# Attention with a gate behind it: the gate's transposes of xs and of its logits issued after the scores, its product one step sooner

## The chip, the cores and the metric

One NeuronCore of a Trainium2 chip runs the whole program. The metric is device time in microseconds (us), lower is better; a kernel's time is the median over its runs.

## The reference, cut to what matters

The program is a windowed attention with 32 global tokens per batch, followed by a mixture of experts. Only the attention and the gate's logits touch the change.

```python
s_g  = scale * q_g @ concat(k_g, k_l).T        # global queries see all keys
out_g = softmax(s_g) @ concat(v_g, v_l)
s_ll = where(|i - j| <= 32, scale * q_l @ k_l.T, -1e9)
s_l  = concat(scale * q_l @ k_g.T, s_ll)       # local queries: window + global keys
out_l = softmax(s_l) @ concat(v_g, v_l)
x = concat(out_g, out_l) as (4608, 512)        # 8 batches, 8 heads, 512 + 32 rows, head size 64
logits = x @ w_gate                            # (4608, 8)
# tokens are assigned to 8 experts greedily by logit, 576 each; out = relu(x @ w1[e]) @ w2[e]
```

## The kernel before

**Attention in steps.** The list `steps` has 40 entries of two units each (the two heads of a pair). A batch b has four local steps 5b to 5b+3 and one global step 5b+4; in the last batch, b = 7, the global step stands second (step 36). The loop of line 468 issues, for each step i, what STEADY (line 415) lists: S, the scores of step i+2 (line 215, or 286 for a global step); T0 and T1, the transposes ("turns") of the probabilities p of step i on TensorE (line 182), each with its copy from PSUM to SBUF on ScalarE (`take`, evac class "p"); M0 and M1, mask and row minimum on VectorE and the exp on ScalarE for step i+2; O0 and O1, the products with v of step i-1 (line 191) and their normalisation on VectorE into `xs[b]`; and G, whatever `extra` holds for the step. Each engine runs its own instructions in this order.

**The gate.** For each batch, `xs[b]` (128 x 4 x 512) is transposed in four groups of four 128x128 turns (`gate_x`, line 318), each group into one PSUM tile and from there copied to `xt` on VectorE (evac class "x"). `gate_m` (line 325) multiplies `xt` by the gate's weights (TensorE, eight instructions), and ScalarE copies the product to `ltc` (class "l"). `gate_l` (line 334) turns `ltc` back (four turns), and VectorE sums four partial results into the logits `L`. All these stand in G, behind O1: with s0 = 5(b+1), the groups of xs in steps s0 to s0+3, the product in s0+4, the turns of the logits in s0+5. Batch 6 (`fast`) has its groups in pairs in steps 35 and 36, its product in step 37 and its logits in 38. Batch 7 has an order of its own. `turn_xg` does the same for the global rows, in G of step s0+1.

**PSUM.** Eight banks: three tiles named S (scores), three named T and two named O. T serves the turns of p (one per unit in a local step, two per unit in a global one), the gate's groups, its product and the turns of the logits, `turn_xg`, and, when the scores of a global step are made, also the small score block `sb` of its second unit (line 290: one S and one T). This `sb` is read by M1's reduction and exp of that step. A T tile goes to a bank whose former tile has had its last reader issued, and the first write then waits for that reader.

**Loads and stores.** They are issued by `piece` (line 437) from the SyncE queue, at a pace set by the estimated work of TensorE (`tick`) and by `now_`, the position within the step; each waits for the last TensorE instruction issued before it. After attention the routing and the expert matmuls follow, which need all logits.

Of the kernel before, what the change touches and what calls it, by code (L numbers as in the profile page):

```python
# [13 lines left out]
ALU = mybir.AluOpType  # L14
AX = mybir.AxisListType
# [4 lines left out]
S = SL + SG  # L20
# [25 lines left out]
@with_exitstack  # L46
def block(ctx, tc, A, out, nbatch=B, dump=None):
    nc = tc.nc
    ctx.enter_context(tc.manual_schedule())
    consts = ctx.enter_context(tc.tile_pool(name="consts", bufs=1))  # L50
    dram = ctx.enter_context(tc.tile_pool(name="dram", bufs=1, space=DRAM))
    xd = dram.tile([N, DM], F32, name="xd")

    ident = consts.tile([128, 128], F32, name="ident")
    L = consts.tile([128, 34, E], F32, name="L")
    if dump is not None:
        nc.vector.memset(L, 0.0)
    rt = Routing(tc, A, consts, L, ident) if out is not None else None
    if rt:
        rt.begin(ctx)  # L60
    attention(tc, A, consts, xd, ident, L, nbatch, rt)
    if dump is not None:
        nc.sync.dma_start(dump["L"], L.rearrange("p a b -> p (a b)"))
        nc.sync.dma_start(dump["x"][:nbatch * S], xd[:nbatch * S])
    if out is not None:
        rt.begin_ps(ctx)
        experts(tc, A, xd, ident, rt, out)
# [3 lines left out]
def attention(ctx, tc, A, consts, xd, ident, L, nbatch, rt=None):  # L71
    nc = tc.nc
# [238 lines left out]
    def evac(dst, src, k):  # L311
        nev[k] += 1
        if who[k][nev[k] % len(who[k])] == "A" and not (k == "p" and nev[k] <= 2):
            nc.scalar.activation(dst, src, AF.Copy)
        else:
            nc.vector.tensor_copy(dst, src)

    def gate_x(src, xt, c, spare):
        t = ps.tile([128, NB, 128], F32, name="S" if spare else "T", bufs=3 if spare else 3)
        n = src.shape[1]  # L320
        for k in range(n):
            pe.transpose(t[:, k, :], src[:, k, c * 128:(c + 1) * 128], ident)
        evac(xt[:, c, :n * 128], t[:, :n].rearrange("p a b -> p (a b)"), "l" if late[0] else "x")

    def gate_m(xt, n):
        lt = ps.tile([128, 512], F32, name="T", bufs=3)
        for c in range(4):
            pe.matmul(lt[32 * c:32 * c + 32, :n * 128], wg[:, c, :], xt[:, c, :n * 128],
                             start=True, stop=True)
        ltc = wk.tile([128, 512], F32, name="ltc", bufs=2)  # L330
        evac(ltc[:, :n * 128], lt[:, :n * 128], "l")
        return ltc

    def gate_l(ltc, J, n):
        t = ps.tile([128, NB, 4, 32], F32, name="T", bufs=3)
        for k in range(n):
            pe.transpose(t[:, k].rearrange("p a b -> p (a b)"), ltc[:, k * 128:(k + 1) * 128], ident)
        nc.vector.tensor_reduce(L[:, J:J + n, :], t[:, :n, :, 0:8].rearrange("p k c e -> p k e c"),
                                axis=AX.X, op=ALU.add)

    def gate_d(xt, c):
        if c == 0:
            lt.append(ps.tile([128, NB, E], F32, name="T", bufs=3))
        for k in range(NB):
            pe.matmul(lt[0][:, k], xt[:, c, 128 * k:128 * k + 128], wg[:, c, 0:E], start=(c + k == 0), stop=(c + k == 6))
        if c == 3:
            nc.scalar.activation(L[:, 4 * nbatch - 4:4 * nbatch], lt[0], AF.Copy)
# [3 lines left out]
    def gate_units(b, src, J, n):  # L351
        xt = []

        def go(c):
            if c == 0:
                xt.append(wk.tile([128, 4, 128 * n], F32, name=f"xt{n}", bufs=1))
            if c < 4:
                gate_x(src(), xt[0], c, b == nbatch - 1)
            elif b == nbatch - 1:
                gate_d(xt[0], c - 4)  # L360
            elif c == 4:
                xt.append(gate_m(xt[0], n))
            else:
                gate_l(xt[1], J, n)
        return [lambda c=c: go(c) for c in range(8 if b == nbatch - 1 else 6)]

    late = [False]
    gxt = {}

    def turn_xg(b):  # L370
        if b % 4 == 0:
            gxt[b // 4] = wk.tile([128, 4, 128], F32, name="xt1", bufs=1)
        t = ps.tile([128, NB, 128], F32, name="S" if b == nbatch - 1 else "T", bufs=3)
        pe.transpose(t[:, 0, :], xg[b].rearrange("p a b -> p (a b)"), ident)
        q = 32 * (b % 4)
        evac(gxt[b // 4][:, :, q:q + 32], t[:, 0].rearrange("p (a b) -> p a b", a=4), "l" if late[0] else "x")

    def gate_g(i):
        gxt[i] = gate_m(gxt[i], 1)
# [8 lines left out]
    extra = {}  # L388

    def put(i, slot, f):  # L390
        extra.setdefault((i, slot), []).append(f)
    for b in range(nbatch):
        last = b == nbatch - 1
        s0 = 5 * (b + 1)
        put(s0 - 2 if last else s0 + 1, 0, lambda b=b: turn_xg(b))
        if b % 4 == 3:
            put(s0 - 1 if last else s0 + 3, 0, lambda b=b: gate_g(b // 4))
            put(s0 if last else s0 + 4, 0, lambda b=b: gate_l(gxt[b // 4], 32 + b // 4, 1))
        lo = gate_units(b, lambda b=b: xs[b], 4 * b, NB)
        if last:  # L400
            put(s0 - 3, 0, lo[0])
            put(s0 - 1, 0, lo[1])
            put(s0, 0, lo[2])
            for f in [lo[4], lo[3]] + lo[5:]:
                put(s0, 2, f)
        else:
            fast = b == nbatch - 2
            for k in range(4):
                put(s0 + (k // 2 if fast else k), 0, lo[k])
            put(s0 + (2 if fast else 4), 0, lo[4])  # L410
            put(s0 + (3 if fast else 5), 0, lo[5])

    LA = 2
    RAMP = 2
    START, STEADY = "T0 T1 O0 O1 S M0 M1 G", "S T0 T1 M0 M1 O0 O1 G"

    need, left = {}, {}
    for i, u in enumerate(steps):
        for q in [u[0].q] if isinstance(u[0], Local) else range(NP):
            for f, t in ((load_qk, i - LA), (load_v, i + 1)):  # L420
                k = f, u[0].b, q
# [8 lines left out]
    def used(f, u):  # L430
        for q in [u[0].q] if isinstance(u[0], Local) else range(NP):
            left[f, u[0].b, q] -= 1
            live[f] -= left[f, u[0].b, q] == 0

    now_ = [-LA]
# [32 lines left out]
    for i in range(-LA, ns + 1):  # L468
        if rt and i == 4:
            rt.load()  # L470
        if rt and i == 9:
            rt.prepare()
        nx = steps[i + LA] if i + LA < ns else []
        cur = steps[i] if 0 <= i < ns else []
        old = steps[i - 1] if i > 0 else []
        if i < RAMP:
            order = START
        else:
            order = STEADY
        late[0] = i >= ns - 1  # L480
        for n, what in enumerate(order.split()):
            now_[0] = i + n / 8
            if what == "S" and nx:
                (local_scores if isinstance(nx[0], Local) else glob_scores)(nx)
                used(load_qk, nx)
            if what[0] == "T" and cur:
                cur[int(what[1])].turn()
                cur[int(what[1])].take()
            if what[0] == "M" and nx:
                nx[int(what[1])].mask()  # L490
                nx[int(what[1])].exp()
            if what[0] == "O" and old:
                old[int(what[1])].out()
                if what[1] == "1":
                    used(load_v, old)
                old[int(what[1])].norm()
            if what == "G":
                if rt and i == ns:
                    for _ in first:
                        pass  # L500
                    rt.digits(slice(0, 28))
                for slot in range(3):
                    for f in extra.get((i, slot), []):
                        f()


WARM = 10
# [789 lines left out]
```

## Time and profile before

| | us |
|---|---|
| median of 3 runs | 689.69 (685.83 to 692.7) |
| profiled execution, its own time | 693.05 |
| its span, first to last instruction | 691.3 |
| PE (TensorE) busy | 644.5 (93%) |
| DVE (VectorE) busy | 460.0 (67%) |
| ACT (ScalarE) busy | 307.4 (44%) |
| POOL (GpSimd) busy | 247.7 (36%) |

Attention takes the span's first 200 us or so; the rest is routing and experts. In the profile, PE is TensorE's matmuls and PEld its weight loads; a transpose is a matmul with `ident`. "T<-ident,p" are the turns of p, "T<-ident,xs" those of xs, "T<-xt,wg" the gate's product, "T<-ident,ltc" the turns of the logits. "[0.47 <-ACT pgt]" behind an instruction is idle time of its engine just before it and what ended it; "issue" is idle time in which the engine waited for nothing that the profile shows. "x8" is a run of eight merged instructions. In such a run the duration is from the first start to the last end, and matmuls overlap, so the distance between two starts says how long a group holds TensorE.

### The profile page before, as it was taken

What the parts mean: (1) busy time and instruction counts of PE and PEld (TensorE: products, weight loads), DVE (VectorE), ACT (ScalarE), POOL (GpSimd) and SP (SyncE); (2) the same over time, 40 slices, a digit from 0 to 9 for tenths busy, and PEclk for the clock granted to TensorE, in tenths of its full rate; (3) what the DMA queues carried; (4) which work ended last, traced back from release to release, by engine and by line L of the source; (5) the groups of instructions that cost most, each with busy time, mean ns of one, the idle gap of its engine ahead of it and who ended that gap; (6) DMA issues with size and microseconds to landing.
All of it is one profiled execution on the core that took longest, in us unless ns stands there. A gap on an engine that the chain in (4) does not pass through costs nothing.

```text
span 691.3 us, 24695 instructions
## 1 busy us (share of the span) xinstructions
PE 644.5 (93%) x10358; PEld 539.5 (78%) x10358; DVE 460.0 (67%) x1765; ACT 307.4 (44%) x828; POOL 247.7 (36%) x313
## 2 busy tenths in 40 slices
PE   7898999999973799999999999999999999999996
PEld 6576777776762698779879879878978978988985
DVE  4688888788776699778758758767767772640410
ACT  5777867876720252443433324334333342542410
POOL 4687767786500311511421331141151133412011
PEclk9999999999985799999999999999999999999999
DMA  8677778876210531713240450361343146431001
GB/s 252 192 241 221 228 227 249 256 212 185 90 68 2 186 124 42 287 47 109 84 168 18 153 190 33 126 197 53 122 125 129 45 142 214 163 127 49 14 15 51
DMA packets 41119, 93.91 MB, mean 136 GB/s; under 512 B 5424, under 2 KB 28208, under 8 KB 36912
## 3 DMA queue, kind: packets, MB, share of 16 engines
q0 software_dynamic: 10240, 51.39, 21.5%
q1 hardware_dynamic: 30768, 40.95, 19.5%
q8 instruction: 81, 1.33, 0.8%
q14 instruction: 30, 0.25, 0.1%
HBM read 74.49 MB, written 17.83 MB: 134 GB/s over the span
## 4 chain that ended last, share of the span: by engine, by line
PE 89%; DVE 4%; issue 3%; DMA 2%; ACT 1%; SPq 0%; POOL 0%; POOLq 0%; ACTq 0%
PE H L1127 28%; PE Y L1086 27%; PE T L90 11%; PE S L90 7%; PE O L90 7%; PE R L630 4%; PE H L965 2%; PE Y L1094 2%; DMA qk<-in_qk_dram 1%; DVE r_pm L552 1%; DMA mask<-in_mask_dram 1%; DMA xg<-xd,idx 0%; DVE r_G L552 0%; DVE r_ce L552 0%; DMA out_dram<-y,idx 0%
## 5 line engine op out<-in xcount | busy, mean ns | idle before, releaser
L1127 PE MATMUL H<-xh,w1h 128*128 128x272 f32 (+2 forms) x512 | 151.1, 295 | 2.4 <-ACT xh L970 2.0
L1127 PE MATMUL H<-xh,w1l 128*128 128x272 f32 (+2 forms) x512 | 150.4, 294 | 0.0
L1127 PE MATMUL H<-xl,w1h 128*128 128x272 f32 (+2 forms) x512 | 149.7, 292 | 0.1
L975 POOL DMA_INDIRECT out_dram<-y,idx x40 | 41.4, 1036 | 183.3 <-ACT y L1074 102.8
L1086 PE MATMUL Y<-w2l,hh 128*128 128x512 f32 x256 | 103.3, 403 | 0.8 <-issue 0.8
L1129 ACT ACTIVATE hh<-H 128x272 fp32r<-128x272 f32 (+2 forms) x128 | 50.8, 398 | 119.7 <-PE H L1127 117.0
L1086 PE MATMUL Y<-w2h,hh 128*128 128x512 f32 x256 | 104.0, 406 | 0.0
L1086 PE MATMUL Y<-w2h,hl 128*128 128x512 f32 x256 | 103.4, 404 | 0.0
L1127 PEld LDWEIGHTS H<-xh,w1h 128*128 128x128 f32 x512 | 97.0, 189 | 3.9 <-ACT xh L970 2.1
L1127 PEld LDWEIGHTS H<-xl,w1h 128*128 128x128 f32 x512 | 97.0, 189 | 1.0 <-DVE xl L552 0.4
L1127 PEld LDWEIGHTS H<-xh,w1l 128*128 128x128 f32 x512 | 97.0, 189 | 0.4
L126 POOL COPY vw<-vw 32x650 f32<-32x650 f32 x96 | 69.4, 723 | 51.6 <-DMA vw<-in_vw_dram 36.1
L180 ACT ACTIVATE p<-p,nm 128x128 f32<-128x128 f32 x256 | 78.0, 397 | 8.1 <-DVE nm L175 8.1
L1074 ACT ACTIVATE y<-Y 128x512 f32<-128x512 f32 (+1 forms) x40 | 21.3, 534 | 123.7 <-PE Y L1086 80.3
L552 DVE SCALAR_TENSOR_TENSOR hl<-H,hh 128x272 fp32r<-128x272 f32 (+2 forms) x128 | 55.1, 434 | 30.3 <-ACT h L1131 18.5
L175 DVE CUSTOM_DVE_ANT_0 p<-S,mask 128x128 f32<-128x128 f32 x256 | 56.5, 286 | 23.3 <-PE S L90 21.8
L90 PE MATMUL S<-qk 64*32 64x128 f32 (+2 forms) x2240 | 52.6, 293 | 9.5 <-issue 5.1
L552 DVE TENSOR_TENSOR w2l<-w2r,w2h 128x512 fp32r<-128x512 f32 x64 | 42.8, 682 | 25.3 <-ACT w2h L931 25.3
L918 POOL DMA_INDIRECT xg<-xd,idx x40 | 43.3, 1082 | 38.1 <-DVE idx L552 23.8
L1086 PEld LDWEIGHTS Y<-w2h,hh 128*128 128x128 f32 x256 | 48.2, 188 | 10.4 <-issue 1.4
L1086 PEld LDWEIGHTS Y<-w2h,hl 128*128 128x128 f32 x256 | 48.2, 188 | 9.8 <-issue 0.5
L1086 PEld LDWEIGHTS Y<-w2l,hh 128*128 128x128 f32 x256 | 48.2, 188 | 9.5 <-issue 0.4
(179 smaller groups left out, 1116.9 us busy)
## 6 DMA issues: line engine op xcount, KB each, us to landing
qk<-in_qk_dram SPq DMA_DIRECT2D x64, 204.0 KB, 2.9
vw<-in_vw_dram SPq DMA_DIRECT2D x64, 162.5 KB, 3.4
xd<-xs SPq DMA_DIRECT2D x28, 256.0 KB, 3.5
qk<-in_qk_dram SPq DMA_DIRECT2D x32, 200.0 KB, 3.0
xd<-xs SPq DMA_DIRECT2D x1, 1024.0 KB
xg<-xd,idx POOLq DMA_INDIRECT x40
out_dram<-y,idx POOLq DMA_INDIRECT x40
vw<-in_ve_dram SPq DMA_DIRECT2D x32, 16.2 KB, 3.0
```

Source lines behind the costliest of these rows:

```text
L90: s.last = op(o, w, x, **kw)
L126: copy(bv[32 * g:32 * g + 32], av[32 * g + 32:32 * g + 64])
L175: nc.vector.tensor_tensor_reduce(s.p[:, c, :], s.st[:, c, :], mask[:, c, :], -SCALE, BIG, ALU.add, ALU.min, s.nm[:, c:c + 1])
L180: nc.scalar.activation(s.p[:, c, :], s.p[:, c, :], AF.Exp, bias=s.nm[:, c:c + 1], scale=-1.0)
L552: return op(*args, **kw)
L630: s.nc.tensor.matmul(out, *args, **kw)
L918: nc.gpsimd.indirect_dma_start(out=dst, out_offset=None, in_=src, element_offset=off, in_offset=bass.IndirectOffsetOnAxis(ap=idx, axis=0))
L975: nc.gpsimd.indirect_dma_start(out=out4 if t == 4 else out, out_offset=bass.IndirectOffsetOnAxis(ap=rt.idx[ph][:, k:k + 1], axis=0), in_=y ...
L1074: nc.scalar.activation(y, p[:, :w], AF.Copy)
L1086: nc.tensor.matmul(p, h[:, f, q], w[f], start=(f + k == 0), stop=(f + k == 9))
L1127: nc.tensor.matmul(p, w[d][:, fs], x[:, d, q], start=(d + k == 0), stop=(d + k == 5))
L1129: nc.scalar.activation(hh[:, f, q], p, AF.Relu)
```

## The change

The order of a step becomes S X T0 T1 M0 Y M1 O0 O1 G. At X the turns of a group of xs, or of the logits, are issued on TensorE; their copy (or sum) on VectorE is returned as a function and called at Y, between the masks of the two units. The product of a batch moves from G of step s0+4 to G of s0+3, and the turns of the logits from G of s0+5 to X of s0+4. In batch 6 the first group of each pair goes to X and the second stays in G; its logits are turned at X of step 38. The position `now_` is counted in tenths of a step instead of eighths.

```diff
--- before.py
+++ after.py
@@ -320,7 +320,8 @@
         n = src.shape[1]
         for k in range(n):
             pe.transpose(t[:, k, :], src[:, k, c * 128:(c + 1) * 128], ident)
-        evac(xt[:, c, :n * 128], t[:, :n].rearrange("p a b -> p (a b)"), "l" if late[0] else "x")
+        k = "l" if late[0] else "x"
+        return lambda: evac(xt[:, c, :n * 128], t[:, :n].rearrange("p a b -> p (a b)"), k)
 
     def gate_m(xt, n):
         lt = ps.tile([128, 512], F32, name="T", bufs=3)
@@ -335,8 +336,8 @@
         t = ps.tile([128, NB, 4, 32], F32, name="T", bufs=3)
         for k in range(n):
             pe.transpose(t[:, k].rearrange("p a b -> p (a b)"), ltc[:, k * 128:(k + 1) * 128], ident)
-        nc.vector.tensor_reduce(L[:, J:J + n, :], t[:, :n, :, 0:8].rearrange("p k c e -> p k e c"),
-                                axis=AX.X, op=ALU.add)
+        return lambda: nc.vector.tensor_reduce(L[:, J:J + n, :], t[:, :n, :, 0:8].rearrange("p k c e -> p k e c"),
+                                               axis=AX.X, op=ALU.add)
 
     def gate_d(xt, c):
         if c == 0:
@@ -355,13 +356,13 @@
             if c == 0:
                 xt.append(wk.tile([128, 4, 128 * n], F32, name=f"xt{n}", bufs=1))
             if c < 4:
-                gate_x(src(), xt[0], c, b == nbatch - 1)
+                return gate_x(src(), xt[0], c, b == nbatch - 1)
             elif b == nbatch - 1:
                 gate_d(xt[0], c - 4)
             elif c == 4:
                 xt.append(gate_m(xt[0], n))
             else:
-                gate_l(xt[1], J, n)
+                return gate_l(xt[1], J, n)
         return [lambda c=c: go(c) for c in range(8 if b == nbatch - 1 else 6)]
 
     late = [False]
@@ -406,13 +407,13 @@
         else:
             fast = b == nbatch - 2
             for k in range(4):
-                put(s0 + (k // 2 if fast else k), 0, lo[k])
-            put(s0 + (2 if fast else 4), 0, lo[4])
-            put(s0 + (3 if fast else 5), 0, lo[5])
+                put(s0 + (k // 2 if fast else k), 0 if fast and k % 2 else "X", lo[k])
+            put(s0 + (2 if fast else 3), 0, lo[4])
+            put(s0 + (3 if fast else 4), "X", lo[5])
 
     LA = 2
     RAMP = 2
-    START, STEADY = "T0 T1 O0 O1 S M0 M1 G", "S T0 T1 M0 M1 O0 O1 G"
+    START, STEADY = "T0 T1 O0 O1 S M0 M1 G", "S X T0 T1 M0 Y M1 O0 O1 G"
 
     need, left = {}, {}
     for i, u in enumerate(steps):
@@ -479,7 +480,12 @@
             order = STEADY
         late[0] = i >= ns - 1
         for n, what in enumerate(order.split()):
-            now_[0] = i + n / 8
+            now_[0] = i + n / len(order.split())
+            if what == "X":
+                turned = [f() for f in extra.get((i, "X"), [])]
+            if what == "Y":
+                for f in turned:
+                    f()
             if what == "S" and nx:
                 (local_scores if isinstance(nx[0], Local) else glob_scores)(nx)
                 used(load_qk, nx)
@@ -501,7 +507,9 @@
                     rt.digits(slice(0, 28))
                 for slot in range(3):
                     for f in extra.get((i, slot), []):
-                        f()
+                        f = f()
+                        if f:
+                            f()
 
 
 WARM = 10
```

## Rows read from the trace of the kernel before

**Rows 1.** The chain that ended last, from 40 to 200 us, by line.
```profile
by line: PE T L90 42.5%; PE O L90 25.9%; PE S L90 24.3%; issue 5.7%; ACT pt L314 0.6%; ACT p L180 0.5%; ACT pgt L314 0.4%; ACTq L314 0.0%
```

**Rows 2.** Waits of PE, 40 to 200 us: total, times, longest.
```profile
PE S L90 <- issue: 4.1, 3, 1.6
PE O L90 <- issue: 3.2, 7, 0.9
PE T L90 <- issue: 1.1, 2, 0.6
```

**Rows 3.** Stretches of one batch: length; PE, PEld, DVE, ACT, POOL busy; clock; DMA.
```profile
43.60:68.20 24.60, 21.80 (x714) 16.74 (x713) 21.83 (x130) 18.66 (x57) 18.25 (x28) 1.00 0.80 241
...
92.50:114.90 22.40, 21.34 (x714) 16.75 (x713) 18.45 (x107) 18.02 (x55) 15.18 (x24) 1.00 0.81 241
```

**Rows 4.** Timeline of PE over steps 17 to 20: start, duration, instructions.
```profile
92.50 1.12 PE L90 MATMUL S<-qk 64*32 64x64 f32 x24
...
93.61 1.09 PE L90 MATMUL T<-ident,p 128*128 128x128 f32 x8
94.63 1.11 PE L90 MATMUL O<-vw,pt 128*32 128x65 f32 x64
95.67 0.66 PE L90 MATMUL T<-ident,xs 128*128 128x128 f32 x4
96.26 1.26 PE L90 MATMUL S<-qk 64*32 64x128 f32 x64
...
100.11 1.21 PE L90 MATMUL S<-qk 64*32 64x128 f32 x64
101.25 1.78 PE L90 MATMUL T<-ident,pg 128*128 128x128 f32 x12
...
103.89 1.04 PE L90 MATMUL T<-xt,wg 128*32 128x512 f32 x8
104.86 1.18 PE L90 MATMUL S<-qk 64*32 64x128 f32 x64
```

**Rows 5.** Timeline of ACT over the same steps.
```profile
94.30 1.09 ACT L314 ACTIVATE pt<-T 128x512 f32<-128x512 f32 x2 [0.40 <-PE T L90]
95.29 0.66 ACT L244 ACTIVATE pg<-S,gm 128x480 f32<-128x480 f32 x1
...
95.92 0.32 ACT L246 ACTIVATE pg<-S,gm 128x64 f32<-128x64 f32 x1
...
103.44 2.44 ACT L180 ACTIVATE p<-p,nm 128x128 f32<-128x128 f32 x8
105.78 0.59 ACT L314 ACTIVATE ltc<-T 128x512 f32<-128x512 f32 x1
```

**Rows 6.** Timeline of step 34: ACT, then PE.
```profile
171.16 0.87 ACT L314 ACTIVATE pgt<-T 128x512 f32<-128x512 f32 x2 [0.29 <-PE T L90]
...
170.47 0.87 PE L90 MATMUL T<-ident,pg 128*128 128x128 f32 x6
171.82 0.88 PE L90 MATMUL T<-ident,pg 128*128 128x128 f32 x6 [0.47 <-ACT pgt L314]
```

**Rows 7.** Timeline around step 38: ACT, then PE.
```profile
190.19 0.58 ACT L314 ACTIVATE ltc<-T 128x512 f32<-128x512 f32 x1
...
190.44 1.04 PE L90 MATMUL T<-ident,p 128*128 128x128 f32 x8
```

**Rows 8.** Stretches from the start to two "issue" gaps, and the gaps on PE's timeline.
```profile
0.00:62.20 62.20, 52.02 (x1615) 40.21 (x1615) 43.50 (x277) 42.52 (x128) 40.14 (x64) 0.97 0.75 224
0.00:66.80 66.80, 55.89 (x1742) 43.44 (x1743) 46.97 (x299) 45.05 (x135) 44.42 (x70) 0.97 0.75 226
...
62.52 0.44 PE L90 MATMUL T<-ident,ltc 128*128 128x128 f32 x2 [0.62 <-issue]
...
67.17 0.43 PE L90 MATMUL O<-vw,pt 128*32 128x65 f32 x15 [0.78 <-issue]
```

**Rows 9.** Waits of DVE, 40 to 200 us: total, times, longest.
```profile
DVE ls L202 <- PE O L90: 6.6, 14, 0.8
```

## The prediction

> **What bounds the kernel now.** I read the profile's page first, then the chain that ended last over the attention stage, the waits of each engine there, and at the end the timelines of single steps. The change touches attention alone, so only the first 200 us count.
>
> The chain from 40 to 200 us lies on PE for 93% (turns 42.5, outputs 25.9, scores 24.3), on "issue" for 5.7%, and on ACT for 1.5%; DVE is not in it [rows 1]. So TensorE's stream of instructions sets the time of attention. PE's own waits there are 8.4 us of "issue" in 12 gaps (4.1 + 3.2 + 1.1) [rows 2]; waits for data come to under 1 us. A batch takes 22.4 to 24.6 us, PE is busy for 21.3 to 21.8 of it; DVE for 18.5 to 21.8 and ACT for 18.0 to 18.7 are below that [rows 3].
>
> The reader is to see in the timeline that PE goes from group to group without a wait: scores at 92.50, turns of p at 93.61, outputs at 94.63, turns of xs at 95.67, the next scores at 96.26 [rows 4]. A reorder takes no instruction off this stream. It can win only on waits, of which there are next to none except "issue", and it can lose by making PE wait.
>
> **What the change moves.** Instructions removed and added: none on any engine. Every group costs what it cost: four turns of xs 0.59 us (95.67 to 96.26), the product 0.97 us (103.89 to 104.86) [rows 4]. The loads and stores are paced by PE's work and keep their number and order nearly; counting `now_` in tenths shifts a store's due time by 0.05 of a step, some 0.2 us of a 4 to 5 us step, in which SP's queue waits for PE anyway. I price that at nothing: DMA ends none of PE's matmul waits in that stage. The copy of xs on DVE comes between the two masks instead of behind the norms: same work, same count. The second unit's masks are later by one copy, but their p is turned two steps on, so this is hidden by that distance. What is not free is which PSUM bank a turn gets and what ACT has queued. Four places:
>
> *1. Steps in which a global step's scores are made.* That is step s0+2, which also holds the third group of xs at X: steps 7, 12, 17, 22, 27 and 32, six of them. Before, T tiles alive at the turns of p were `sb` and the two turns. Now the xs tile is alive too, and it is let go only at Y, `sb` only at M1, both behind T1 in the order. T has three banks, so T1 must take T0's and wait for T0's copy on ACT. From rows: the copy begins 0.69 us after the turns begin (93.61 to 94.30), and as two copies take 1.09 and the next instruction begins 0.99 after the first [rows 4, 5], they stand 0.50 apart and one lasts 0.60. T1 starts 1.3 us after T0 instead of 0.51 (half of 1.02): a wait of 0.8 us.
>
> Then ACT is late. T1 ends 1.3 + 0.51 = 1.81 after T0's start, its copy begins 0.18 later, the exps of the global unit 0.50 after that, and the small exp that lets the second S bank go begins 0.63 after them and takes 0.32 [rows 5]: 3.44. Before, the next scores began 0.02 us after this exp ended (96.24, 96.26), because the xs group stood in between [rows 4, 5]. Now outputs are followed at once by scores: PE is there at 1.81 + 1.04 = 2.85 and waits 0.6 us. Together 1.4 us a step, 8.4 us for six.
>
> *2. Turns of the logits at X of step s0+4.* They need `ltc`, whose copy on ACT stands behind the two copies and eight exps of step s0+3. From the start of that step's turns: 0.69 to the first copy, 0.99 to the exps, 2.34 to the copy of `ltc` (103.44 to 105.78) and 0.59 for it [rows 5], 4.6 us. PE needs 1.02 + 1.04 + 0.97 for turns, outputs and product and 1.14 for the scores (100.11 to 101.25) [rows 4], 4.2 us. Wait: 0.45 us, and T0, T1 and all behind them queue on it; six steps (9, 14, 19, 24, 29, 34), 2.7 us. Before, these turns stood a step later and had cover. In step 38 likewise: PE is free at 190.44, `ltc` is there at 190.77 [rows 7], 0.35 us.
>
> *3. Global steps with a tile held at X.* Four T tiles for the turns of pg, two banks left. Step 34 before shows that case, since `sb` is held there: 0.47 us after six of twelve turns [rows 6]. The twelve turns with three banks at 101.25 took 1.78 us; eight take 1.09, and four more at 0.128 each (1.02 for 8) make 1.60 [rows 4], so 0.2 is paid already; 0.3 us more in steps 9, 14, 19, 24, 29 and 36, 1.8 us.
>
> *4. Step 34* now holds `sb` and the logits' tile: one bank for four tiles, three copies waited for. By the distances above, 0.18 + 0.60 + 0.05 twice and 0.18 + 0.37 + 0.05 once (a pair takes 0.87, the second is 0.37 [rows 6]), 2.3 us less the 0.47 paid before: 1.8 us.
>
> Gross: 8.4 + 2.7 + 0.35 + 1.8 + 1.8 = 15 us.
>
> **What gives some of it back.** The "issue" gaps stand at fixed distances: 1615 matmuls to the one before 62.5 us and 1742 to the next [rows 8], 127 apart, with their weight loads 254 instructions; other gaps lie at multiples of that. I read them as the next block of PE's instructions arriving late. Such a gap shrinks by what PE waited for other reasons in the block before. Some 37 blocks run between 40 and 200 us (714 matmuls per batch [rows 3]); 12 end in a gap, of 0.70 us on average [rows 2]. Fourteen places with a new wait (six, six, 36 and 38), each in a block with a chance of 12/37: 14 x 0.32 x 0.7 = 3 us back. Net 12 us.
>
> The Trainium skill (Runtime: NRT & Kernel Launch, "Instruction fetch mechanics") says that instructions stream in 256-instruction blocks and that crossing a boundary is mostly hidden. The distance agrees with the rows, "mostly hidden" does for two in three boundaries. By that rule alone nothing would come back and the sum would be the gross one.
>
> **Bounds.** Place 1 from below: 0.47, the wait that step 34 shows [rows 6], and no wait at the scores; place 2 nothing, if ACT runs ahead; and all 8.4 us of gaps absorbed: the sum is about zero, 690 us. From above: no gap absorbed, and each copy finds one more ACT instruction of 0.5 us ahead of it, 14 x 0.5: 15 + 7 = 22 us, 711. I take the values that single steps give, as the ACT wait of 0.40 before 94.30 [rows 5] says that ACT stood ready there.
>
> **Rivals.**
> *Banks do not bind.* If T1 found a free bank in those six steps (the moved turns then cost nothing there), scores would come 2.65 after T0's start instead of 2.1: 0.55 x 6 = 3.3, with places 2 and 3 some 8, less 3 for the gaps: +5, 695 us. For it: the rows show no local step with one bank. Against it: three banks and the order of the code. Or the gaps absorb most of the waits; the time is the same. This is also the case in which the change hardly does anything.
> *DVE set the pace.* DVE waits 6.6 us for outputs in 14 places [rows 9]; with a copy between the masks it arrives later and would not wait. If DVE were the bound, those 6.6 us would go: 683 us. Its place are the steps with a group of xs; it decides from the point at which DVE's work in a step is longer than PE's, and then the next scores would wait for masks. Against it: DVE has no share in the chain [rows 1], and is 4 us below the batch's length in the second row [rows 3]; for it, only the first, 21.83 of 24.6.
> *ACT is late everywhere.* The upper bound: 711 us.
>
> **How the numbers follow.** Forecast, +12: 0.60. Upper case: 0.08. Banks do not bind or gaps absorb: 0.22. DVE: 0.10. The sum was made on the profiled execution, 693.05 us (1.75 around the span of 691.3): 705. This execution lies 3.4 above the median of 689.69, so for a median I put 689.69 + 12 = 701.7. About 1%, 6.9 us, is what a measurement can tell from no change. Slower by over 1%: 0.68; within: 0.22; faster: 0.10. The range goes from 690, leaving out the DVE case, to 711; the likeliest case's own is 697 to 708.
>
> **What would show it.** In the timeline after, the turns of p in a step with global scores come as four, a gap of 0.8 us ended by ACT pt, and four; the scores behind them wait some 0.6 us on ACT's exps; turns of ltc wait 0.4 us for ACT; step 34 has three gaps. PE's waits for ACT, under 1 us before, sum to 12 to 15 us, "issue" falls by some 3, and routing begins 12 us later, with all behind it as before. I am wrong if the eight turns stay together, or if the batches' length stays at 22.4 to 24.6 us though they don't.

## The result: 1.28% slower, ten microseconds lost in attention

| | before | after |
|---|---|---|
| median (runs) | 689.64 us (6) | 699.51 us (6) |
| ratio, 95% interval | | 1.0128 (1.0100 to 1.0156) |
| span of the profiled execution | 691.3 us | 698.7 us |
| first matmul of the routing in that execution | 201.98 us | 214.24 us |

The ratio is not the quotient of the two medians, which is 1.0143 and lies in the interval too. The prediction was 701.7 us, in a range of 690 to 711, slower by over 1% with a chance of 0.68. The loss lies in attention. Further profiles, below, put the routing's first matmul at 201.75 to 202.99 us in the kernel before (three profiles) and at 211.95 and 214.24 after (two): on average 10.9 us later. From there to the end, two profiles of the kernel before take 483.4 and 483.9 us and both of the changed kernel 484.3 and 484.5. Only the first profile of the kernel before took longer there, 489.3; the change has no part in that.

The chain that ended last in the changed kernel, from 40 to 200 us, by line; its counterpart is [rows 1]:

```profile
by line: PE T L90 34.0%; PE S L90 20.9%; PE O L90 16.4%; issue 8.6%; ACT p L180 7.3%; ACT pt L314 7.2%; ACT pg L244 2.9%; ACT ltc L314 1.6%; ACT pgt L314 1.5%; ACTq L314 0.1%
```

PE's share has gone from 93% to 71%, ACT's from 1.5 to 20.6%: the chain now runs through ScalarE's copies and exps. The exps (L180) stand in it because the copy of `ltc` is queued behind them. PE's waits, 40 to 212 us, the whole stage (waiting line, what ended it, total, times, longest), against [rows 2]:

```profile
PE S L90 <- issue: 4.9, 4, 2.2
PE T L90 <- ACT pt L314: 4.1, 6, 0.7
PE O L90 <- issue: 4.1, 7, 1.2
PE T L90 <- ACT ltc L314: 2.5, 5, 0.6
PE S L90 <- ACT pg L244: 2.4, 7, 0.3
PE T L90 <- issue: 1.3, 1, 1.3
PE T L90 <- ACT pgt L314: 1.2, 3, 0.5
```

Waits for ACT sum to 10.2 us, under 1 us before. PE's timeline over steps 17 to 19, the same steps as [rows 4] (start, duration, instructions, idle time before and its releaser):

```profile
96.47 1.12 PE L90 MATMUL S<-qk 64*32 64x64 f32 x24
97.33 0.31 PE L90 MATMUL T<-qk 64*32 64x64 f32 x8
97.58 0.66 PE L90 MATMUL T<-ident,xs 128*128 128x128 f32 x4
98.07 0.60 PE L90 MATMUL T<-ident,p 128*128 128x128 f32 x4
99.36 0.66 PE L90 MATMUL T<-ident,p 128*128 128x128 f32 x4 [0.69 <-ACT pt L314]
99.94 1.12 PE L90 MATMUL O<-vw,pt 128*32 128x65 f32 x64
101.40 1.44 PE L90 MATMUL S<-qk 64*32 64x128 f32 x64 [0.34 <-ACT pg L244]
102.77 0.66 PE L90 MATMUL T<-ident,xs 128*128 128x128 f32 x4
103.26 1.04 PE L90 MATMUL T<-ident,p 128*128 128x128 f32 x8
104.22 1.12 PE L90 MATMUL O<-vw,pt 128*32 128x65 f32 x64
105.16 1.04 PE L90 MATMUL T<-xt,wg 128*32 128x512 f32 x8
106.13 1.18 PE L90 MATMUL S<-qk 64*32 64x128 f32 x64
107.90 0.66 PE L90 MATMUL T<-ident,ltc 128*128 128x128 f32 x4 [0.59 <-ACT ltc L314]
108.39 1.73 PE L90 MATMUL T<-ident,pg 128*128 128x128 f32 x12
```

The eight turns of p at 93.61 in [rows 4] are now four, a gap of 0.69 us, and four. From these scores to the next it took 3.76 us before (92.50 to 96.26) and takes 4.93 (96.47 to 101.40). ACT over the same stretch:

```profile
98.70 0.60 ACT L314 ACTIVATE pt<-T 128x512 f32<-128x512 f32 x1 [0.40 <-PE T L90]
100.11 0.60 ACT L314 ACTIVATE pt<-T 128x512 f32<-128x512 f32 x1 [0.81 <-PE T L90]
100.60 0.66 ACT L244 ACTIVATE pg<-S,gm 128x480 f32<-128x480 f32 x1
```

The pair of copies of [rows 5] has come apart: T0's ends at 99.30, T1 begins at 99.36, its copy at 100.11, and the exps that free the score banks only at 100.60.

### The profile page after: what moved, and what is told of

It reads as the page before. It is cut to its first block, busy times and chain, and to the rows that moved or that the text cites. A ratio compares the mean times of both kernels' runs of the same rounds, so it can differ in the third digit from the quotient of the medians.

```text
span 698.7 us, 24674 instructions
## 1 busy us (share of the span) xinstructions
PE 643.8 (92%) x10358; PEld 540.3 (77%) x10358; DVE 460.6 (66%) x1765; ACT 308.4 (44%) x828; POOL 246.9 (35%) x313
## 4 chain that ended last, share of the span: by engine, by line
PE 87%; ACT 5%; DVE 4%; issue 3%; DMA 0%; POOLq 0%; ACTq 0%
PE H L1135 28%; PE Y L1094 27%; PE T L90 10%; PE S L90 7%; PE O L90 5%; PE R L638 4%; PE H L973 2%; PE Y L1102 2%; ACT p L180 2%; ACT pt L314 2%; PE Y L1168 1%; ACT pg L244 1%; DVE r_pm L560 1%; DVE p L175 1%; DVE r_G L560 0%
## 5 line engine op out<-in xcount | busy, mean ns | idle before, releaser
L180 ACT ACTIVATE p<-p,nm 128x128 f32<-128x128 f32 x256 | 78.0, 396 | 9.2 <-DVE nm L175 9.2
L175 DVE CUSTOM_DVE_ANT_0 p<-S,mask 128x128 f32<-128x128 f32 x256 | 58.4, 286 | 28.4 <-PE S L90 25.1
L90 PE MATMUL S<-qk 64*32 64x128 f32 (+2 forms) x2240 | 53.9, 296 | 12.4 <-issue 7.0
```

Of the source, the lines that this page charges most:

```text
L90: s.last = op(o, w, x, **kw)
L175: nc.vector.tensor_tensor_reduce(s.p[:, c, :], s.st[:, c, :], mask[:, c, :], -SCALE, BIG, ALU.add, ALU.min, s.nm[:, c:c + 1])
L180: nc.scalar.activation(s.p[:, c, :], s.p[:, c, :], AF.Exp, bias=s.nm[:, c:c + 1], scale=-1.0)
```

## The experiments

The theory: TensorE waits for PSUM banks and for ACT's queue in the places that the prediction names. The rivals: the copy between the masks holds up DVE; or the new order of TensorE's stream costs by itself, scores now standing right behind outputs, with instructions that come late ("issue").

**Putting the third group back behind the outputs** (steps 7, 12, 17, 22, 27, 32):

```diff
-            put(s0 + (k // 2 if fast else k), 0 if fast and k % 2 else "X", lo[k])
+            put(s0 + (k // 2 if fast else k), 0 if (k % 2 if fast else k == 2) else "X", lo[k])
```

> The changed kernel with only the third group of xs (steps 7, 12, 17, 22, 27, 32) put back behind the outputs. Theory of banks (T1 shares T0's bank while sb and the xs tile are alive, and ACT is late behind it): in these six steps the eight turns of p run together again, PE's waits for ACT pt (4.1 us) and ACT pg (2.4 us) go but for the one of step 34 (0.34 us), the step takes 3.8 us again instead of 4.93, and the time falls by some 6 to 7 us, from 699.5 to about 693 (ratio to before 1.004). Rival, the order itself (scores right behind the outputs make instructions arrive late, issue 8.4 before and 10.3 us after): one group in four of the order is undone, so 2 to 3 us at most, 697. Rival, the copy between the masks delays DVE: the same 2 to 3 us.

Measured: ratio to before 1.0051 (1.0013 to 1.0089). The eight turns stand together again and the waits for `pt` are gone:

```profile
66.99 1.09 PE L90 MATMUL T<-ident,p 128*128 128x128 f32 x8
68.02 1.12 PE L90 MATMUL O<-vw,pt 128*32 128x65 f32 x64
69.06 0.66 PE L90 MATMUL T<-ident,xs 128*128 128x128 f32 x4
69.65 1.29 PE L90 MATMUL S<-qk 64*32 64x128 f32 x64
```

Some 5 us of the loss come from these six groups; an estimate from the two intervals is 2 to 9 us, so the time alone does not exclude the 2 to 3 us of the rivals. The waits decide: those for `pt` went from 4.1 us to none and those for `pg` from 2.4 to 0.3, as the theory says, while "issue" rose from 10.3 to 12.4 us, where the rival of the order wanted less.

**Putting the turns of the logits back**, one step later:

```diff
-            put(s0 + (3 if fast else 4), "X", lo[5])
+            put(s0 + (3 if fast else 5), 0, lo[5])
```

> The changed kernel with only the turns of the logits put back behind the outputs, one step later; the product stays one step sooner. Theory of waits: PE's waits for ACT ltc (2.5 us in five places) go, with them the 0.47 in step 9; step 34 has its 0.47 as before. The six steps with the third group keep their 0.69 and 0.34. Time lower by some 3 us, 696.5 (ratio 1.010). Rival, the order of the instruction stream: no change beyond 1 us, since four turns of 140 instructions move.

Measured: 1.0099 (1.0065 to 1.0134). The waits for `ltc` are gone, those for `pt` (4.1 us) and `pg` (2.4 us) are as they were. The time fell by 0.3%, the size expected, but the intervals of the two overlap.

**Both edits together:**

> The changed kernel with the third group of xs and the turns of the logits both put back behind the outputs; the other groups stay at X with their copies at Y, the product stays one step sooner. Theory of waits: all waits but the 0.47 of step 36 are gone, and the time is that of before within 0.3%: 690 us (ratio 1.000). Rival, the order of the stream or the copy between the masks: half of X is still in place, and 3 to 5 us stay (694).

Measured: 1.0012 (0.9977 to 1.0047). By the time, removing the waits leaves at most 0.5%, though three of four groups are still at X with their copies between the masks, and no wait of PE ends on one of these copies. The product one step sooner and `now_` in tenths are still in this kernel too; neither was tested alone. The profiles show more of the loss than the time does: the routing's first matmul stands at 208.14 and 206.87 us (two profiles), 4 to 6 us later than in the kernel before. The waits of PE, 40 to 200 us, show where:

```profile
PE S L90 <- issue: 6.1, 6, 2.3
PE O L90 <- issue: 5.4, 8, 1.5
PE T L90 <- issue: 1.5, 2, 0.8
PE T L90 <- ACT pgt L314: 0.7, 2, 0.5
PE S L90 <- ACT pg L244: 0.3, 1, 0.3
```

"issue" is 13.0 us, against 8.4 in [rows 2], an excess that no theory here had put at this size.

**The copy ahead of both masks**, so that the xs tile is let go before T1:

```diff
-    START, STEADY = "T0 T1 O0 O1 S M0 M1 G", "S X T0 T1 M0 Y M1 O0 O1 G"
+    START, STEADY = "T0 T1 O0 O1 S M0 M1 G", "S X Y T0 T1 M0 M1 O0 O1 G"
```

> The changed kernel with Y directly behind X: the copy of xs stands ahead of both masks. The xs tile is then let go before T1, which takes its bank instead of T0's. Theory of banks: T1 waits for DVE's copy of xs, not for ACT's of T0: it starts about 0.9 us after T0 instead of 1.29 (0.49 without a wait), the scores behind wait 0.3 to 0.4 us on ACT as now or less; six steps by some 0.4, 2 to 3 us less than 699.5 (ratio 1.010). Rival, DVE sets the pace: the masks of both units come 0.7 us later behind the scores, in all steps with X, and the time rises, by 0.3 to 0.7 in each of some 27 steps (over 705).

Measured: 1.0116 (1.0080 to 1.0153). The mechanism is as said, T1 now waits half as long, and for DVE:

```profile
70.81 0.60 PE L90 MATMUL T<-ident,p 128*128 128x128 f32 x4
71.76 0.66 PE L90 MATMUL T<-ident,p 128*128 128x128 f32 x4 [0.35 <-DVE xt L316]
72.34 1.12 PE L90 MATMUL O<-vw,pt 128*32 128x65 f32 x64
73.80 1.46 PE L90 MATMUL S<-qk 64*32 64x128 f32 x64 [0.34 <-ACT pg L244]
```

The gain of 2 to 3 us does not show in the time: the interval holds both 1.010 and the 1.0128 of the change. Waits other than "issue" fell by 2.2 us, to 8.0, but "issue" is 11.0. DVE as the one that sets the pace (over 705 us) is excluded.

**The same kernels again**, for the scatter of "issue":

> The kernel before once more, for the scatter of the issue gaps of PE between 40 and 200 us (8.4 us in its first profile) and of the stretch between the routing and the first expert matmul. If the gaps are instructions that come late behind other transfers, their places stay at multiples of 127 matmuls and their sum moves by some us from run to run; if the order alone sets them, the sum is 8.4 within 1 us.

> As the run ahead of it, a third profile of the kernel before: issue gaps of 8.4 within 1 us if the order sets them, spread over some us if transfers do.

> The kernel with the third group and the logits put back, once more. Its first profile had 13.0 us of issue gaps, against 8.4 in the kernel before, and no more waits for ACT than that. If scores right behind outputs cost instructions that come late, the sum is again well above those of the kernel before (12 or more against 9 or less); if it is scatter, the two kinds of run overlap.

> The changed kernel once more. PE's waits for ACT (pt 4.1, ltc 2.5, pg 2.4, pgt 1.2 us) come again within 0.5 us each, since they follow from the order and the banks; issue gaps, 10.3 us in its first profile, lie some 3 us under those of e3_again if waits take from them, and anywhere in the scatter if not. The first wait of routing stands some 12 us later than in the two runs of the kernel before of this call, or, by their scatter, 8 to 14.

Measured, PE's waits between 40 and 200 us in all profiles of the kernels so far:

| kernel | issue, us | other, us | what stands between outputs and next scores |
|---|---|---|---|
| before, three profiles | 8.4, 9.0, 8.8 | 0.8, 1.3, 1.8 | the gate's group or its product, in most steps |
| third group and logits in G, two profiles | 13.0, 13.6 | 1.0, 1.1 | the third group, the logits, the product; else nothing |
| third group in G | 12.4 | 3.7 | the third group, the product; else nothing |
| logits in G | 8.6 | 7.6 | the logits, the product; else nothing |
| the change, two profiles | 10.3, 8.7 | 10.2, 10.3 | nothing but the product |
| the change, copy ahead of both masks | 11.0 | 8.0 | nothing but the product |

The waits for ACT came again to 0.2 us. "issue" scatters by 1 to 2 us, but the kernel with both put back, which hardly waits otherwise, lies 4 us or more above three profiles of the kernel before in both of its own, and where TensorE waits for ACT the sum is lower again. So two opposite effects seem to meet: the new order costs late instructions, and waits give them time to arrive.

**Spreading the slow groups**, a test of the first effect in the other direction. This is the kernel before, with only the order string changed:

```diff
-    START, STEADY = "T0 T1 O0 O1 S M0 M1 G", "S T0 T1 M0 M1 O0 O1 G"
+    START, STEADY = "T0 T1 O0 O1 S M0 M1 G", "S T0 M0 O0 T1 M1 O1 G"
```

> The kernel before (all of the gate behind the outputs) with a step's order S T0 M0 O0 T1 M1 O1 G: the slow groups of four turns stand apart between groups of 32 outputs. A block of 127 matmuls then leaves out at most one group of four turns and lasts some 3.1 us or more, where it could be 2.65 with T0 and T1 together, and about 2.15 with the group of xs beside them (e3). Theory that a late block of instructions costs what its arrival exceeds the block before it: issue gaps between 40 and 200 us fall below the 8.4 to 9.0 of the kernel before, to 5 or 6 us, with no new waits for ACT, and the time by 2 to 3 us (ratio 0.996). Rival, the gaps follow the load of the DMA queues alone: 8.5 to 9 us again, ratio 1.000. Rival, ACT: T1's copy now stands behind the exps of the first unit; if outputs of the next step or T's banks wait for it, some 0.5 us a step and a ratio above 1.01.

Measured: "issue" fell to 6.6 us (4.8 + 1.3 + 0.5), no new waits for ACT, nearly the 5 to 6 us of the theory of the gaps; yet the ratio is 1.0027 (1.0002 to 1.0051), which excludes the forecast of 0.996. PE's timeline of one step shows where it went:

```profile
98.35 1.16 PE L90 MATMUL S<-qk 64*32 64x128 f32 x64
99.44 0.66 PE L90 MATMUL T<-ident,p 128*128 128x128 f32 x4
100.02 0.66 PE L90 MATMUL O<-vw,pt 128*32 128x65 f32 x32
100.61 0.66 PE L90 MATMUL T<-ident,p 128*128 128x128 f32 x4
101.20 0.66 PE L90 MATMUL O<-vw,pt 128*32 128x65 f32 x32
101.79 0.66 PE L90 MATMUL T<-ident,xs 128*128 128x128 f32 x4
```

There is no wait in it. But four turns alone hold PE for 0.58 us (99.44 to 100.02), where eight take 1.02, and 32 outputs for 0.59, where 64 take 1.04 [rows 4]. The four groups take 2.35 us (99.44 to 101.79) instead of 2.06: two more changes between turns and outputs cost 0.29 us, some 0.14 each. Part of it comes back in the scores; over the 25 steps of the ledger below, what is neither wait nor gap is 115.2 us here and 110 in the kernel before, 0.2 us a step.

**The same spreading with both masks late:**

```diff
-    START, STEADY = "T0 T1 O0 O1 S M0 M1 G", "S T0 T1 M0 M1 O0 O1 G"
+    START, STEADY = "T0 T1 O0 O1 S M0 M1 G", "S T0 O0 T1 M0 M1 O1 G"
```

> The kernel before with the order S T0 O0 T1 M0 M1 O1 G: the same spreading on TensorE, but both masks and exps stay behind both turns on ACT. Theory of the gaps: they fall as in e5_spread. Theory of banks and ACT: in the seven steps with global scores the small exp ends 1.6 us after T1, while outputs and the group of xs cover 0.52 + 0.59 only, so the next scores wait some 0.5 us, 3.5 us in all, which takes the gain back: ratio 1.001, and 1.005 if the gaps do not fall.

Measured: 1.0265 (1.0231 to 1.0298), worse than either expectation. "issue" fell again (5.7 us), and the scores wait for ACT pg, for 5.9 us where 3.5 were expected. What I had left out is DVE's order: the norm of O0 now stands ahead of both masks, so the masks wait for outputs:

```profile
DVE ls L202 <- PE O L90: 28.3, 23, 2.4
```

Against 6.6 us in [rows 9]. DVE's norms and masks now stand in the chain from 40 to 200 us, with about a tenth of it. PE's waits other than "issue" come to 7.5 us, which does not account for a loss of some 18; where the rest lies was not traced.

**The gate's turns behind the turns of p**, the change otherwise kept:

```diff
-    START, STEADY = "T0 T1 O0 O1 S M0 M1 G", "S X T0 T1 M0 Y M1 O0 O1 G"
+    START, STEADY = "T0 T1 O0 O1 S M0 M1 G", "S T0 T1 X M0 Y M1 O0 O1 G"
```

> The changed kernel with X between T1 and M0: the gate's turns stand behind the turns of p instead of ahead of them, all else as in the change. Theory of banks and ACT: in the six steps with the third group it is now the xs group that takes T0's bank and waits, some 0.3 us (T0's copy ends 1.29 us after T0 begins, T1 ends at 1.0), T1 and its copy are not late, and the next scores find the small exp done (2.65 us after T0's start, while turns, group and outputs take 2.8); the turns of the logits have twelve more turns as cover, so ACT ltc goes. PE's waits other than issue fall from some 10 us to 2 or 3. Issue gaps stay at those of e3 (12 to 13 us), because scores still follow outputs directly and few waits take from them. Ratio to before about 1.003 (1.0128 for the change). Rival, that it is the place of the copy between the masks or the step's new order as a whole that costs: the ratio stays above 1.009.

> The kernel with the gate's turns behind the turns of p once more. Its first profile had 14.2 us of issue gaps, one of them of 3.6 us, and 1.9 us of other waits of PE. If late instructions are what the order with scores right behind outputs costs, the sum is again 11 us or more, against 8.4 to 9.0 in three profiles of the kernel before; if the one long gap was an accident, it is 10.5 or less.

Measured: the waits went as computed, but not the time: 1.0101 (1.0070 to 1.0132). PE's waits in its first profile:

```profile
PE S L90 <- issue: 7.4, 5, 3.6
PE O L90 <- issue: 6.3, 8, 1.7
PE T L90 <- ACT pgt L314: 0.9, 2, 0.5
PE T L90 <- ACT pt L314: 0.8, 3, 0.3
PE T L90 <- issue: 0.5, 1, 0.5
```

Waits other than "issue" are 1.9 us (2.1 in the second profile) instead of 10.2, but "issue" is 14.2 and 13.1 us. Here scores stand right behind outputs as in the change, without the waits that cover it. My forecast of 1.003 took the gaps of the kernel with both put back, which came, and took their cost from that kernel's time, which did not hold: with nearly the same waits and gaps the two kernels lie at 1.0101 and 1.0012. The profiles put them closer, with the routing's first matmul at 209.06 and 210.29 us here, 208.14 and 206.87 there. Why the times differ by more is open.

## Why the prediction was right, point by point

**The bound.** PE's stream sets the time of attention: borne out. The chain had ACT in it only where PE was made to wait, and no wait of PE ended on a copy that had moved between the masks, but for 0.3 us on a sum of logits in the second profile.

**Place 1, turns of p in one bank.** Foreseen T1 1.3 us after T0, measured 1.29 (98.07 to 99.36). Foreseen scores 3.44 to 3.46 us after T0, measured 3.33. The step grew by 1.17 us, not 1.4, in each of six steps: 7 us where 8.4 were put. In the program as built, T0 and T1 have one bank in each of these steps. Taking it away alone gave back about 5 us (1.0128 to 1.0051), as "issue" rose by 2.

**Place 2, logits before their copy.** Foreseen 0.45 us in six steps; measured 0.53 to 0.59 in four, 0.18 in one, and none in step 9, where an "issue" gap of 0.45 us had just delayed the turns. 2.5 us where 2.7 were put. The 0.35 us of step 38 did not come: the turns at 202.65 stand behind a group of xs and have no wait.

**Place 3, global steps.** This term was too large. The 0.47 us came in steps 9 and 36; in steps 14 to 29 the twelve turns ran through in 1.73 us, as at 108.39 above. There, in the program as built, the third of their four tiles has the bank of the logits' tile, and not that of the first. The trace bears it out: the sum that lets the logits' tile go ends at 108.88, the third tile's turns begin at 109.05, and the copy of the first ends only at 109.63. In steps 9 and 36 the third tile has the first one's bank. The step that failed is "Four T tiles for the turns of pg, two banks left": which bank a tile gets is fixed when the program is laid out, and in four of six steps it counts on the sum at Y being done.

**Place 4, step 34.** Wrong for the same reason: 1.8 us were put, for four tiles in one bank; in the program as built they have two, one of them that of the logits' tile. PE's timeline of the changed kernel has one gap there, shorter than the 0.47 of [rows 6]:

```profile
182.27 0.66 PE L90 MATMUL T<-ident,ltc 128*128 128x128 f32 x4 [0.59 <-ACT ltc L314]
182.76 0.98 PE L90 MATMUL T<-ident,pg 128*128 128x128 f32 x6
184.05 0.88 PE L90 MATMUL T<-ident,pg 128*128 128x128 f32 x6 [0.30 <-ACT pgt L314]
```

**The gaps that give back.** Foreseen "issue" down by 3 us; it stayed (8.4 to 9.0 before, 8.7 and 10.3 after). The mechanism was there, but a cost of the same kind that I had not counted stands against it. Without the waits, the order with scores right behind outputs has 13 to 14 us of gaps; with them 8.7 to 10.3. So, by these sums, about 4 us were given back, and about 5 were added first. I had reasoned that a reorder takes nothing off the stream and so could lose by waits alone.

What the gaps are can be read from the transfers that the traces hold. The page has a queue of its own for instructions (packets, MB, share of 16 engines):

```profile
q8 instruction: 81, 1.33, 0.8%
```

The line is the same in all 14 profiles, and each of the 81 packets has 16,384 bytes; 10358 matmuls and as many weight loads are 127 of each to a packet. All 171 "issue" gaps of the 14 profiles between 40 and 200 us stand at about multiples of 127 matmuls, the one at matmul 2378, give or take three, in every profile, and each ends 1.0 to 1.7 us after a packet of this queue has ended. At moments drawn at random from the stretch, the last packet ended that long ago in about one of six. So the gaps are instructions that arrive late, as the prediction read them.

Take the 127 matmuls between two such places as a block. Half of the blocks that end in a gap last 4.1 to 4.7 us with it, though their matmuls need as little as 2.2: how slow and fast groups follow each other sets how much of the arrival is covered. The block that ends at matmul 2378 has 3.17 us of work in the kernel before and a gap of 1.6 to 2.2; with the slow groups spread 3.80 and 0.46; with the gate's turns behind the turns of p 2.48 and 2.5 to 3.6. The longest gap of all, 3.6 us, follows a packet that began 3.8 us after the first matmul of the block in front of the gap, where the median of the 171 is 1.8; why it began late is not shown.

**"Every group costs what it cost".** Also wrong, by little and to the good. Turns of xs next to the turns of p take 0.49 + 0.97 us (102.77 to 104.22), where apart they took 0.59 + 1.02 [rows 4]: 0.15 us less in each step with X, since one change between kinds of matmul falls away. The spreading run shows the same with the other sign, 0.14 us for each change added.

**The ledger.** From the scores of step 7 to those of step 32, five batches of the same instructions:

| | length, us | issue | other waits | rest |
|---|---|---|---|---|
| before, three profiles | 118.0, 119.8, 120.0 | 7.9, 8.6, 8.6 | 0.3, 0.8, 1.3 | 109.8, 110.4, 110.1 |
| the change, two profiles | 124.6, 125.9 | 7.9, 7.9 | 7.5, 7.6 | 109.2, 110.4 |

The whole difference of 6 us is in the waits other than "issue", which but for 0.3 us in one profile all end on ACT; "issue" falls by 0.5 and the rest is level (in it, shorter turns and longer, partly waiting scores cancel). The remainder of the 10.9 us lies in steps 32 to 34 (9.7 us instead of 7.7 to 8.0), in the steps behind (33.5 and 33.7 instead of 32.1 to 32.6) and in the scatter of the first 45 us.

**The sum.** 12 us net were put, 9.9 came. Places 1 and 2 carried it. The gross sum of 15 us was too large by some 5, of them some 3 in places 3 and 4, and the 3 us that the gaps were to give back did not come on balance. The two errors have opposite signs; that the total hit closer than its terms is luck. Two signs missed accordingly: waits for ACT of 12 to 15 us (10.2 came) and three gaps in step 34 (one came).

**The rivals.** Free banks: no, the split turns are in every one of the six steps. DVE as the pace: no, PE's waits on DVE come to nothing in one profile of the change and 0.3 us in the other. ACT late everywhere: no, ACT stood idle ahead of each copy (0.40 and 0.81 us above). None of the kernels tried is faster than the one before.

## What to carry to other kernels

Before moving work ahead in a saturated stream, list which tiles are alive at each place of the new order, count them against the banks, look up in the built program which bank each one has, and follow the copies that free them through the queue of the engine that makes them: here a fourth tile for three banks cost 1.2 us each time, while a count alone put 3.6 us on places that cost 0.7. A stream that is full has no free place, though: the order also decides how often the kind of matmul changes and how densely instructions follow, and a wait removed can come back as a gap in the stream. Take the steps apart in experiments, and read sums of waits and of "issue" side by side, since either can hide in the other.

## What the runs showed of the hardware

Each change between turns (128x128 tiles) and outputs (128x32) costs PE some 0.14 us that no wait shows: turns and outputs in four groups take 2.35 us, in two groups 2.06, and four turns next to eight save 0.15. The product, which has the outputs' tile shape, follows 64 outputs after 0.94 us (104.22 to 105.16), where turns follow after 1.04 [rows 4]. The Trainium skill (TensorEngine Tiling (Array Packing), Key Properties) says that changing the tiling mode drains TensorE; the runs agree, with these numbers beside it, but none tested the shape apart from the operation.

TensorE's instructions came in packets of 16,384 bytes, one for some 127 matmuls with their weight loads, and 171 gaps at these places ended 1.0 to 1.7 us after a packet's end. The gaps, the longest of 3.6 us, depend on the order of the stream: 5.7 and 6.6 us in 160 with the slow groups spread, 8.4 to 9.0 in the kernel before, 13 to 14 with the densest order and few other waits.
